# Who asks for the output stores of the lower tiles: GpSimd in place of SyncE

## The chip, the cores and the metric

The kernel runs on one core of a Trainium2 chip. The time of a run is the time on the device, in microseconds. It was run three times before the change: the median is 1073.89 us, the lowest 1072.86 and the highest 1074.72. One execution was also recorded by the hardware profiler; that one took 1074.23 us, and the profile that is read below is of that execution.

The core has engines that run their own instruction streams in order and wait for each other on semaphores: PE (TensorE, matrix products), DVE (VectorE), ACT (ScalarE), POOL (GpSimd) and SP (SyncE). In this kernel SP computes nothing, it only asks for transfers (DMAs). ACT and POOL can ask for them too. The transfers themselves run on the core's 16 DMA engines.

## The reference

Eight sequences (B) of 576 tokens (S), eight heads (H) of 64 (D), all in float32. Attention is confined to chunks of 64 tokens. Its output is mixed by the real part of a two-dimensional Fourier transform, added to itself, normalised, and sent through an MLP of 512 to 2048 to 512 without biases:

```python
scores = scale * np.matmul(q_c, k_c.transpose(0, 1, 2, 4, 3))      # per chunk of 64 tokens
attn = np.exp(scores - max); attn = attn / (sum(attn) + 1e-09)
x = (attn @ v_c)            # regrouped to (8, 576, 512)
u = x + np.real(fft(fft(x, axis=1), axis=2))
un = (u - mean(u)) / np.sqrt(var(u) + 1e-06)
out = u + np.maximum(un @ w_ch1, 0.0) @ w_ch2
```

## The kernel before, in words

**Tiles.** The 576 tokens of a sequence are nine chunks of 64. A tile holds 128 tokens. For the Fourier transform over the tokens, chunks are paired from both ends: a LO tile (lower) holds two chunks of the first half of a sequence, a HI tile holds the mirrored chunks of the second half, and a RE tile holds the middle chunks of two sequences. So there are 16 LO tiles, 16 HI tiles and 4 RE tiles. Rows within a tile are ordered by odd and even tokens, for the LO tiles from the end of a chunk to its start.

**Groups.** The MLP goes over nine groups (`g` from 0 to 8). Groups 0 to 7 hold the four tiles of one sequence, in the order LO, HI, LO, HI (`groups[g]`). The last group holds the four RE tiles. While PE works on the MLP of a group, the attention and the Fourier mix of the next sequence (`attention(b)`, `fourier(b)`) are woven in between as side work, step by step at due times, in the loop at the end of the kernel.

**The order.** Every instruction stands in the order in which the program text issues it (`tc.manual_schedule`); nothing is moved by a planner. Each engine takes its own instructions in that order.

**The MLP.** Group 0 uses the weights as they are (`up_first`, `down_plain`). Later groups multiply in halves of 256 with seven products in place of eight (`up_halves`, L1265, whose matmuls are line 1289, and `down_halves`, L1319, whose matmuls are line 1341). The combinations of weights that this needs are made once, kept in DRAM (`s1`, `s2`, `s3`), and fetched slab by slab (`fetch`, L1151: L1155 for the first product's weights, L1160 for the second's, 1 MB each). For group 1 they are made in place by POOL: `keep1`, line 1069, four operations for each of four pairs of weight blocks, in the steps that begin at the end of group 0. The last group has its own products (`down_few`), and POOL makes their weights in `make_rest` (line 1133).

**The ends of a group.** In group 0 all four tiles are finished in the last step of `down_plain`: DVE adds the residual (L1249) and `store` (L1030) is called. In groups 1 to 7, `down_halves` finishes the tiles in four steps: the first LO tile and then the first HI tile after the sixth product (`o == 5`, DVE at L1358), the second LO tile and then the second HI tile after the seventh (DVE at L1361). The outputs lie in `os_`, a part of the weight buffer `wb` that is shared with `xs`, an operand of the next group (written by DVE at L1167).

**The store.** For each of a tile's two chunks `store` asks for the DMAs that bring its rows back into the order of tokens:

- a LO tile: one DMA for each chunk, 64 rows of 2 KB, 128 KB, at line 1037. Since rows are kept in the order odd and even, from the end, the DRAM side is written as two interleaved sequences of 32 rows: its sizes are 2 x 32 x 512.
- a HI tile: two DMAs for each chunk, 32 rows each, 64 KB, line 1046, one by SP and one by ACT.
- a RE tile: lines 1040 to 1042.

**What shares SP with it.** SP also loads q and k (`load`, L250, four DMAs for a tile) and v (`load_v`, L273), fetches the slabs, and keeps `s1` (`keep1_store`, L1074). The loaded q and k are transposed by DVE (L416, into `qT` and `kT`) before PE makes the scores (L448); for a LO tile POOL then copies a column of `qT` (L418). The attention's output is divided by its sum by DVE (L511 to L515), and a few of its rows are moved by POOL (`shift`, L555; L526).

**Completion semaphores.** The DMAs that SP and ACT ask for share eight completion semaphores, taken in turn in the program's order. So one such DMA can be issued only after the eighth one before it has landed. The DMAs that POOL asks for have eight of their own. The groups before the last put twelve stores into the rotation of SP and ACT: four of LO tiles (SP), four of HI tiles by SP and four by ACT.

Of the kernel before, what the change touches and what calls it, by code (L numbers as in the profile page):

```python
# [16 lines left out]
def kernel(  # L17
# [32 lines left out]
    nc = tc.nc  # L50
# [3 lines left out]
    CH = 64  # L54
# [140 lines left out]
    def kind(n):  # L195
        return tiles[n][0]
# [4 lines left out]
    def chunks(n):  # L201

        what, b, i = tiles[n]
        if what == RE:
            return [(b, NC // 2), (b + 1, NC // 2)]
        if what == LO:
            return [(b, 2 * i), (b, 2 * i + 1)]
        return [(b, NC - 1 - 2 * i), (b, NC - 2 - 2 * i)]
# [821 lines left out]
    def store(n, o):  # L1030

        last = n in groups[-1][1::2]
        for h, (b, c) in enumerate(chunks(n)):
            r0, t0 = h * CH, c * CH
            if kind(n) == LO:
                to = out[b, t0 + 1:t0 + CH + 1, :][::-1].rearrange("(i r) d -> r i d", r=2)[::-1]
                nc.sync.dma_start(out=to, in_=o[r0:r0 + CH])
            elif kind(n) == RE:
                eng = nc.scalar if last and h else nc.sync
                eng.dma_start(out=out[b, t0 + 1:t0 + CH:2, :], in_=o[r0:r0 + ODD])  # L1040
                eng.dma_start(out=out[b, t0 + 4:t0 + CH:2, :], in_=o[r0 + ODD + 2:r0 + CH])
                eng.dma_start(out=out[b, 0:t0 + 3:t0 + 2, :], in_=o[r0 + ODD:r0 + ODD + 2])
            else:
                for r in range(2):
                    eng = nc.scalar if r else nc.sync
                    eng.dma_start(out=out[b, t0 + 1 - r:t0 + CH:2, :], in_=o[r0 + ODD * r:r0 + ODD * r + ODD])
# [182 lines left out]
    def down_plain(g, h1):  # L1229
# [4 lines left out]
        for m in range(KF):  # L1234
            for s, dn in enumerate(dns):
                nc.tensor.matmul(  # L1236
                    out=dn,
                    lhsT=h1[:, m, s * 128:(s + 1) * 128],
                    rhs=w2[:, m, :],
                    start=(m == 0),  # L1240
                    stop=(m == KF - 1),
                )
                if m == KF - 1:
                    n = groups[g][s]
                    if s < G - 1:
                        o = three_p.tile([128, DM], FP32, tag="o", name="o")
                    else:
                        o = one_p.tile([128, 2 * (HM + 1)], FP32, tag="two", name="o")[:, 0:DM]
                    nc.vector.tensor_tensor(out=o, in0=dn, in1=natural(n), op=ALU.add)  # L1249
                    store(n, o)  # L1250
            for j in range(G):
                due = KF - (G - j + 1)
                if m == due - 2:
                    normed(g + 1, j)
                if m == due:
                    turned(g + 1, j)
                    if j >= 2 and g + 1 >= first_of[1]:
                        combined(g + 1, j - 2)
            yield
# [59 lines left out]
    def down_halves(g, h1):  # L1319
        pas, pbs = {}, {}  # L1320
        for o in range(NO):
            w = slab2[((g - first_of[2]) * NO + o) % NS2]
            for r in range(2):
# [21 lines left out]
                if o == 0:  # L1345
                    nc.scalar.copy(a, dst)
                elif o == 1:
                    nc.vector.tensor_tensor(out=b, in0=dst, in1=a, op=ALU.add)
                elif o == 2:
                    nc.vector.tensor_tensor(out=a, in0=dst, in1=b, op=ALU.add)  # L1350
                elif o == 3:
                    nc.vector.tensor_tensor(out=ohigh[:, HM:DM], in0=dst, in1=ohigh[:, HM:DM], op=ALU.add)
                    nc.gpsimd.tensor_tensor(out=olow[:, HM:DM], in0=b, in1=natural(low)[:, HM:DM], op=ALU.add)
                    nc.gpsimd.tensor_tensor(out=ohigh[:, 0:HM], in0=b, in1=natural(high)[:, 0:HM], op=ALU.add)
                elif o == 4:
                    nc.vector.tensor_tensor(out=olow[:, 0:HM], in0=dst, in1=natural(low)[:, 0:HM], op=ALU.add)
                elif o == 5:
                    nc.vector.tensor_tensor(out=olow[:, HM:DM], in0=dst, in1=olow[:, HM:DM], op=ALU.add)  # L1358
                    store(low, olow)
                else:  # L1360
                    nc.vector.tensor_tensor(out=ohigh[:, 0:HM], in0=dst, in1=ohigh[:, 0:HM], op=ALU.add)  # L1361
                    store(high, ohigh)
# [254 lines left out]
```

## Time and profile before

| what | value |
|---|---|
| median of three runs | 1073.89 us |
| the profiled execution | 1074.23 us |
| its span (first to last instruction) | 1072.2 us |
| PE busy | 1046.3 us, 98% |
| DVE busy | 610.8 us, 57% |
| POOL busy | 406.6 us, 38% |
| ACT busy | 315.3 us, 29% |
| HBM traffic | 177.31 MB read, 34.08 MB written, 197 GB/s over the span |
| SP's and ACT's DMAs | 208.04 MB and 2.76 MB |
| POOL's DMAs | 0.66 MB |

The profile is of one execution. Busy time leaves out the instructions that only issue DMAs, which is why SP has no row. The span is 2.0 us shorter than the profiled execution's time; that part lies before the first and after the last instruction. Line numbers (L1037) are those of the kernel. In the list of waits a line says which engine and operation waited, for whom, and then the microseconds in total, how often, and the longest. In a timeline the first number is the start in microseconds from the start of the span, the second the length, and the end of the line, in brackets, is how long the engine was idle before and what ended it. In the chain of waits, each piece is followed back from the last instruction to what released it.

### The profile page before, as it was taken

To read this page: it belongs to the slowest core of one execution; us is meant where nothing else is said; L and a number is where in the kernel's file an instruction comes from. 1 tells how busy PE (TensorE), PEld (TensorE's weight loads), DVE (VectorE), ACT (ScalarE), POOL (GpSimd) and SP (SyncE) were. 2 spreads that over 40 slices of the span, in tenths; PEclk is the share of its full clock that TensorE was granted. 3 is DMA by queue.
4 is the path that set the end of the run, shared out by engine and by line. 5 is a ranking of instruction groups with operands and counts; after the bars stand their busy time and mean duration, and the time that the engine had idled before them with its cause. 6 is when DMAs were issued, how large, how long until landed. Compare 5 with 4: busy or idle time off the path is not lost.

```text
span 1072.2 us, 20212 instructions
## 1 busy us (share of the span) xinstructions
PE 1046.3 (98%) x7498; PEld 854.6 (80%) x7498; DVE 610.8 (57%) x1319; ACT 315.3 (29%) x746; POOL 406.6 (38%) x531
## 2 busy tenths in 40 slices
PE   8999989899999999999999999999999999999997
PEld 6645444688888888888888888788888888888886
DVE  4798986684567465664565554745664535433331
ACT  4688563233113411322032312331133103101200
POOL 4310018672415140344134321614161726780281
PEclk9999999999999999999999999999999999999999
DMA  8767565489668546883667266954654559776763
GB/s 176 232 186 218 123 196 189 139 249 312 233 199 232 149 140 198 239 232 119 191 209 231 99 182 195 231 165 163 202 177 116 208 191 350 229 231 199 272 228 106
DMA packets 157759, 212.74 MB, mean 198 GB/s; under 512 B 69308, under 2 KB 103100, under 8 KB 151390
## 3 DMA queue, kind: packets, MB, share of 16 engines
q1 hardware_dynamic: 154012, 208.04, 63.4%
q10 hardware_dynamic: 3330, 2.76, 1.1%
q8 instruction: 60, 0.98, 0.4%
q0 software_dynamic: 320, 0.66, 0.3%
q14 instruction: 37, 0.30, 0.1%
HBM read 177.31 MB, written 34.08 MB: 197 GB/s over the span
## 4 chain that ended last, share of the span: by engine, by line
PE 77%; DVE 8%; DMA 5%; ACT 4%; SPq 3%; issue 2%; POOL 1%; DVEq 0%; ACTq 0%; POOLq 0%
PE pa L1289 19%; PE pb L1341 18%; PE pb L1289 14%; PE pa L1341 13%; PE dn L1405 4%; PE pt L397 2%; PE mix L838 2%; DMA xall<-in_moe_w_ch_dram 1%; SPq L263 1%; PE xp L498 1%; PE z L719 1%; DVE power L378 1%; DMA out_dram<-o 1%; PE sc L448 1%; DMA v<-in_v_dram 1%
## 5 line engine op out<-in xcount | busy, mean ns | idle before, releaser
L1289 PE MATMUL pa<-unT,wa 128*128 128x256 f32 x736 | 175.0, 381 | 2.5 <-DVE wa L1297 2.5
L1289 PEld LDWEIGHTS pa<-unT,wa 128*128 128x128 f32 x736 | 138.3, 190 | 21.8 <-DVE wa L1297 2.7
L1289 PE MATMUL pb<-wa 128*128 128x256 f32 x448 | 106.9, 381 | 0.1
L1341 PE MATMUL pa<-wb,h 128*128 128x256 f32 x448 | 101.5, 380 | 0.0
L1341 PE MATMUL pb<-wb,h 128*128 128x256 f32 x448 | 100.7, 379 | 0.0
L1289 PEld LDWEIGHTS pb<-wa 128*128 128x128 f32 x448 | 84.1, 190 | 12.3 <-DVE h L1299 0.5
L1341 PEld LDWEIGHTS pa<-wb,h 128*128 128x128 f32 x448 | 83.9, 190 | 11.3
L1341 PEld LDWEIGHTS pb<-wb,h 128*128 128x128 f32 x448 | 84.1, 190 | 11.0
L1169 POOL TENSOR_TENSOR h<-h 128x256 f32<-128x256 f32 x56 | 47.7, 860 | 102.3 <-DVE wb L1167 98.2
L555 POOL COPY xall<-xall 1x512 f32<-1x512 f32 x28 | 17.8, 636 | 154.3 <-DVE xall L515 126.9
L1295 DVE TENSOR_TENSOR wa<-pb,wa 128x256 f32<-128x256 f32 x56 | 23.8, 425 | 69.7 <-ACT wa L1294 69.7
L1289 PE MATMUL pb<-unT,wa 128*128 128x256 f32 x256 | 60.5, 379 | 0.0
L1303 ACT ACTIVATE h<-pa 128x256 f32<-128x256 f32 x64 | 24.6, 384 | 114.1 <-PE pa L1289 113.6
L1236 PE MATMUL dn<-wb,h 128*128 128x512 f32 x128 | 57.5, 597 | 0.0
L1294 ACT COPY wa<-pa 128x256 f32<-128x256 f32 x56 | 20.9, 372 | 123.5 <-PE pa L1289 80.6
L1289 PEld LDWEIGHTS pb<-unT,wa 128*128 128x128 f32 x256 | 48.6, 190 | 6.6
L1289 PE MATMUL pa<-wa 128*128 128x256 f32 x224 | 53.9, 383 | 0.0
L1309 ACT ACTIVATE h<-h 128x512 f32<-128x512 f32 x64 | 39.6, 629 | 45.0 <-DVE h L1308 44.8
L1341 PE MATMUL pb<-wb,yall 128*128 128x256 f32 x224 | 51.2, 381 | 0.0
L1341 PE MATMUL pa<-wb,yall 128*128 128x256 f32 x224 | 50.6, 379 | 0.3 <-DMA wb<-s 0.3
L1341 PE MATMUL pb<-wb 128*128 128x256 f32 x224 | 50.7, 379 | 0.0
L1195 PE MATMUL up<-unT,wa 128*128 128x512 f32 x108 | 49.4, 598 | 0.0
(299 smaller groups left out, 1976.1 us busy)
## 6 DMA issues: line engine op xcount, KB each, us to landing
wb<-s SPq DMA_DIRECT2D x49, 1024.0 KB
wa<-s SPq DMA_DIRECT2D x196, 256.0 KB
xall<-in_moe_w_ch_dram SPq DMA_DIRECT2D x22, 512.0 KB
q<-in_q_dram SPq DMA_DIRECT2D x96, 112.0 KB
k<-in_k_dram SPq DMA_DIRECT2D x96, 112.0 KB
wb<-s SPq DMA_DIRECT2D x16, 512.0 KB
v<-in_v_dram SPq DMA_DIRECT2D x124, 64.0 KB
s<-part SPq DMA_DIRECT2D x30, 256.0 KB
```

Of the source, the lines that this page charges most:

```text
L397: nc.tensor.transpose(pt[:, j, :], src(j), ident)
L838: nc.tensor.matmul(out=mix[:, cols], lhsT=zt[:, T], rhs=tab, start=(T == 0), stop=(T == 3), skip_group_check=True,)
L1169: nc.gpsimd.tensor_tensor(out=h1[:, m, hi], in0=h1[:, m, lo], in1=h1[:, m, hi], op=ALU.subtract)
L1195: nc.tensor.matmul(out=up, lhsT=w1[:, kk, m * 128:(m + 1) * 128], rhs=unT[:, kk], start=(kk == 0), stop=(kk == KD - 1), skip_group_check=True,
L1236: nc.tensor.matmul(out=dn, lhsT=h1[:, m, s * 128:(s + 1) * 128], rhs=w2[:, m, :], start=(m == 0), stop=(m == KF - 1),)
L1289: nc.tensor.matmul(out=dst, lhsT=w[:, kk, r], rhs=rhs[o][:, kk], start=(o in (0, 1) and kk == 0), stop=(kk == 1), skip_group_check=True,)
L1294: nc.scalar.copy(a, dst)
L1295: nc.vector.tensor_tensor(out=b, in0=pbs[r][:, 0], in1=a, op=ALU.add)
L1303: nc.scalar.activation(out=h1[:, m, lo], in_=dst, func=ACTF.Relu)
L1309: nc.scalar.activation(out=h1[:, HF + m], in_=h1[:, HF + m], func=ACTF.Relu)
L1341: nc.tensor.matmul(out=dst, lhsT=lhs[:, m], rhs=w[:, m], start=(o in (0, 2) and m == 0), stop=(m == HF - 1), skip_group_check=True,)
L1405: nc.tensor.matmul(out=dst, lhsT=lhs[:, m], rhs=w[:, m], start=(fresh and not half and m == 0), stop=(m == 3), skip_group_check=True,)
```

## The change

The DMA that stores a chunk of a LO tile is issued by GpSimd (POOL) in place of SyncE. What it transfers, from where and to where, is the same. The stores of HI and RE tiles stay as they are.

```diff
@@ -1034,7 +1034,7 @@
             r0, t0 = h * CH, c * CH
             if kind(n) == LO:
                 to = out[b, t0 + 1:t0 + CH + 1, :][::-1].rearrange("(i r) d -> r i d", r=2)[::-1]
-                nc.sync.dma_start(out=to, in_=o[r0:r0 + CH])
+                nc.gpsimd.dma_start(out=to, in_=o[r0:r0 + CH])
             elif kind(n) == RE:
                 eng = nc.scalar if last and h else nc.sync
                 eng.dma_start(out=out[b, t0 + 1:t0 + CH:2, :], in_=o[r0:r0 + ODD])
```

There are 16 LO tiles of two chunks, so 32 DMAs change their engine, four in each of the groups 0 to 7. They leave SP's instruction stream and the rotation of eight completion semaphores that SP and ACT share, and stand in POOL's stream at the place where `store` is called; they use POOL's own completion semaphores. The order of the instructions on PE, DVE and ACT is the same as before.

## The prediction

> **What bounds the kernel now.** I read the page first. TensorE (PE) is busy for 98% of the span at full clock, so a change that only moves who issues a DMA can win no more than the time in which PE stands still and the store is the reason. The page also shows that POOL, the engine that receives the work, has room.
>
> ```profile
> span 1072.2 us, 20212 instructions
> PE 1046.3 (98%) x7498; PEld 854.6 (80%) x7498; DVE 610.8 (57%) x1319; ACT 315.3 (29%) x746; POOL 406.6 (38%) x531
> ```
>
> Second, the waits from the first changed store (about 189 us) to the end. Only these three of PE are long:
>
> ```profile
> PE pa L1289 <- DVE wa L1297: 2.5, 1, 2.5
> PE pb L1289 <- POOL wb L1069: 2.4, 1, 2.4
> PE sc L448 <- DVE kT L416: 0.7, 1, 0.7
> ```
>
> I also took PE's starts in order and counted what each gap has over the usual spacing. The same places cost 2.66 us (at 670.4 us), 2.78 (189.8) and 0.88 (211.4), and then 0.42 (218.8), 0.74 (222.5) and 0.41 (260.7) follow; nothing else after 189 us is over 0.3. The 2.78 ends in front of the first changed store and stays. So at most 0.88 + 0.42 + 0.74 + 0.41 + 2.66 = 5.1 us can be won.
>
> Third, what stands behind those gaps. The chain of waits around 200 us, and around 660 us, in order of time (start, length, what):
>
> ```profile
> 195.48 7.65 DMA out_dram<-o
> 203.15 0.34 SPq L250
> ...
> 204.01 7.00 DMA k<-in_k_dram
> ...
> 211.13 0.06 DVE kT L416
> ```
>
> ```profile
> 657.88 8.90 DMA v<-in_v_dram
> 666.78 0.02 issue
> 666.80 4.80 DMA q<-in_q_dram
> ...
> 671.80 0.06 DVE qT L416
> ```
>
> A store (`out_dram<-o`, L1037) takes 7.65 us to land, a load of k waits for it and itself takes 7.00, and DVE's transpose waits for the load. The timeline of SP around 655 us shows how the second chain starts:
>
> ```profile
> 649.78 5.84 SPq L1037 DMA_DIRECT2D out_dram<-wb  x2
> 655.72 0.83 SPq L1046 DMA_DIRECT2D out_dram<-wb  x2
> 656.65 0.38 SPq L1160 DMA_DIRECT2D wb<-s  x1
> 657.13 3.59 SPq L273 DMA_DIRECT2D v<-in_v_dram  x4
> 662.40 4.77 SPq L250 DMA_DIRECT2D q<-in_q_dram  x4
> ```
>
> Two stores take 5.84 us of SP because the second waits for a landing, and everything behind it on SP is late by that. DVE's timeline gives the end of both chains, with its idle time in brackets:
>
> ```profile
> 211.13 1.09 DVE L416 STREAM_TRANSPOSE kT<-k 128x512 f32<-128x512 f32 x1 [3.74 <-DMA k<-in_k_dram]
> 671.80 1.09 DVE L416 STREAM_TRANSPOSE qT<-q 128x512 f32<-128x512 f32 x1 [4.12 <-DMA q<-in_q_dram]
> ```
>
> **What the Trainium skill says.** All of this is on its page "DMA: Bandwidth & Descriptors". (1) "Why a DMA increments its semaphore by 16 and not by 1": a DMA uses k engines, the largest k up to 16 that divides the outermost sizes of both sides, and on SP's path always the lowest-numbered k. The lower store's DRAM side is 2x32x512, so k = 2. The trace agrees: each L1037 moves its semaphore in 3 steps, all other DMAs of SP in 16, and while only L1037 is in flight the 16 engines are about 0.1 busy at 12 to 18 GB/s. It lands in 6.90 us in the median (5.29 to 10.43), the upper stores of 64 KB each (L1046) in 5.65. Loads of k issued behind lower stores took 7.0 to 7.9 us, others with none ahead (217.74 to 219.37) 2.6 to 2.9. From POOL, the section says, either such DMAs go to all 16 engines or to k engines that rotate; no trace here shows which. (2) "Queues, rings and completion order": each queue has its own ring on each engine, and an engine alternates between rings. So a store in POOL's ring no longer stands ahead of SP's loads in one line, though it still shares the engine. (3) "Issuing engines are not separate DMA queues": the bytes run on the same 16 engines, so nothing is won in bandwidth. (4) "Specifications": the first byte comes after about 1 us from POOL against 0.6 from SP. That is less than the landing spread here, and nobody waits for these stores but their buffers (below).
>
> **The change part by part.**
>
> *Removed.* 32 DMAs leave SP, 4 in each of the 8 full groups: about 0.52 us each (28 with median 0.520, four with 0.582), together 17 us of SP's issue time, plus 28 us of waiting in front of them (the largest entries are 19.9 for DVE L1358 and 11.2 for landings). SP isn't the bound on average, so this counts only where SP's next load is late.
>
> *Moved past.* SP's and ACT's DMAs share eight completion semaphores in rotation, so each waits until the eighth before it has landed. A group's stores put 12 DMAs into that rotation before, 8 after. Each wait now falls on another DMA. I worked out the pairs from the program's order.
>
> At 195 to 211 us (end of group 0): before, k waits for the store issued at 195.48 (landed 203.14), is issued at 203.15 to 204.01, and lands at 210.05 to 211.01. After, its slots belong to q loads landed by 196.6, so DVE's release of the old k at about 198.4 decides: issued 198.4 to 200, and at 3 to 5 us landed about 203. DVE was free for it at 207.4, so its 3.74 us of idle time goes. The next work on DVE, L511, needs attention's output from PE (210.9 to 211.5), so DVE doesn't gain 3.7 us but the transpose's 1.09, run earlier. PE's 0.88 goes with it; of the 0.42 and 0.74, which come from DVE's backlog, a part. Bounds 0.9 and 2.0; I take 1.2.
>
> At 649 to 671 us (end of group 4): after, the upper stores stand where the lower ones stood, at 649.8. The second waits for a slab fetch issued at 647.14 (fetches land in 4.64 to 9.21, median 5.24; so about 652.5). Then fetch at 653, v at 653.5 to 656, q at 657.5 to 659.5, landed about 664. DVE could take it at 671.80 - 4.12 = 667.7, so 3.7 us of margin, and the stall of 2.66 goes whole. If that fetch takes 9.2 us, q comes 4 us later and about 0.3 of the stall is left.
>
> At 260.7 us a slab is late by 0.41 because SP issues without a pause from 244 to 257. With four DMAs less in that group SP runs ahead; I take 0.3 (0 to 0.41).
>
> *Added.* 32 DMA issues on POOL. Its only direct row is
>
> ```profile
> L273 POOL DMA_DIRECT2D v<-in_v_dram x10 | 6.3, 633 | 0.6 <-DMA v<-in_v_dram 0.4 <-issue 0.2
> ```
>
> so 0.63 us each, 32 x 0.63 = 20 us, on an engine 38% busy. That row is of another shape, so I bound one issue by 0.5 (SP's) and 1.5 us. Behind them in POOL's order:
> - Group 0: four DMAs stand between two sets of L1069. What PE needs of the set behind them was ready at 198.13, is ready 4 x 0.63 = 2.5 us later, at 200.6, and is used by PE at 207.33. Cover 207.33 - 198.13 = 9.2 us, gone above 9.2/4 = 2.3 us for each DMA.
> - Groups 1, 3, 5: four DMAs before row copies (L555). The last wait (DVE L1361) ends at 306.5, so POOL is free at 307.8, three copies of 0.64 end at 309.7, and the fourth waits for DVE until 312.07 anyway. Cover 2.3 us, then 15 us of idle time (L526, to 329.08).
> - Groups 2, 4: two DMAs ahead of a small copy for qT (638.7), which PE uses at 648.7; two ahead of copies that wait for 650.34 (POOL is through with the DMAs at 646.5, with the first two copies at 648). Cover 10 and 2 us.
> - Groups 6, 7: between additions (L1133) for the last group; POOL's next work that PE needs is at 997. Cover over 10 us.
>
> So this adds 0 to PE within my bounds.
>
> *Waits added.* POOL now waits for DVE's L1358 and L1361, in the groups above, and what is queued behind is what I listed. The lower rows' buffer is rewritten by DVE (L1167) at 331.5, 444.9, 892.6 and so on; a store issued by 307.8 with even 10.4 us to land is through by 318.2. Cover 13 us. The end of the kernel has no such store.
>
> *Sum.* 1.2 + 2.66 + 0.3 = 4.2 us. The profiled execution took 1074.23 (span 1072.2 plus 2.0 around it), so 1070.0. The median is 1073.89, 0.34 lower, so **1069.7 us**.
>
> **The rivals.**
>
> *The gain is taken back by the rotation (no change).* With SP running earlier, another DMA takes the place of the store in a wait: the slab fetch of 647.14, or upper stores of 9 to 10 us. Then only group 0's 1.2 us are won, or a new gap of 1 to 2 us eats the rest: 1074.23 - 1.2 = 1073.0 in the profile, 1072.7 as median. For it: eight semaphores still serve q, k, v, slabs and upper stores, and fetches have a long tail. Against it: 3.7 us of margin.
>
> *POOL's issue is dear (slower).* POOL could need several microseconds for a DMA while DVE is busy beside it. For it: two additions of one size, L1169 and L1353 (128x256), take 860 and 725 ns, so POOL's pace isn't constant. At 4 us each, four cost 16 us, which is 16 - 9.2 = 6.8 us of PE at group 0; groups 1, 3 and 5 lose nothing more (what their copies lack is followed by 15 idle us). Against the 4.2 won that is +2.6, so 1073.89 + 2.6 = 1076.5. It decides from (9.2 + 4.2)/4 = 3.4 us a DMA up. Against: the row with 0.63, which is five times less.
>
> *The transfers matter, not the issue.* If two engines are clogged as before, whoever asks, loads behind stay at 7 us. Then at group 0 k still starts 4 us earlier and lands 207; at group 4 q lands at about 667.5: nearly the same gain, 3.7 us, 1070.2. It lies in the forecast's range.
>
> **How the numbers follow.** Forecast with the third rival: 0.66, range 1068.3 to 1071.3 (bounds 0.9 + 2.4 + 0 = 3.3 and 2.0 + 2.66 + 0.41 = 5.1 us, plus 0.7 for other small gaps and the runs' spread). Taken back: 0.18, 1071.7 to 1075. Dear issue, or one new stall of that size: 0.16, 1076 to 1080. The kernel's measurement tells 0.2%, or 2.15 us, from no change: faster means below 1071.7, slower above 1076.0. For 8 in 10 the range takes the first and the second case: 1068.0 to 1075.5.
>
> **What would show it.** Right: at 200 to 211 us k is issued before 201 and DVE's idle time before kT is gone; at 670 us PE's wait for L1297 is gone; the POOL DMAs of L1037 are at 0.5 to 1 us; L1069 moves by 2.5 us without a wait of PE. Wrong: a PE wait for POOL's L1069 near 207, a wait on the slab fetch at 650, or a new late slab in the groups' first halves, where SP's earlier loads meet slab fetches.

## The result, and the profile after

The changed kernel took 1071.53 us in the median of ten runs (1068.75 to 1073.07), beside 1073.99 us for the kernel before in ten runs (1071.62 to 1076.28). The ratio is 0.997, with a 95% interval of 0.996 to 0.998: 2.5 us faster. Forecast were 1069.7 us, 4.2 us faster. The time lies in the stated range and on the stated side, but the gain is six tenths of what was forecast. Repeated later in 14 runs, the changed kernel took 1070.69 us beside 1073.70, ratio 0.9974 (0.9964 to 0.9984).

The profiled execution of the changed kernel took 1068.75 us, with a span of 1067.0. That is 5.5 us under the profiled execution of before, more than twice the difference of the medians. Why the two profiles differ by more than the kernels do is a main finding below.

The page of the kernel after, first lines:

```profile
span 1067.0 us, 20226 instructions
PE 1044.8 (98%) x7498; PEld 854.8 (80%) x7498; DVE 610.8 (57%) x1319; ACT 315.4 (30%) x746; POOL 429.6 (40%) x563
```

POOL has 32 instructions more (531 to 563) and 23.0 us more busy time (406.6 to 429.6). PE, DVE and ACT have as many instructions as before. Of PE's three long waits after 189 us, one is left in the list of waits:

```profile
PE pb L1289 <- POOL wb L1069: 2.4, 1, 2.4
```

It is the one in front of the first changed store, 2.78 us over the usual spacing as before. The timeline of SP around the end of group 4 (start, length, what) shows how the chain that began with two stores of 5.84 us has gone:

```profile
647.31 2.25 SPq L1046 DMA_DIRECT2D out_dram<-wb  x2
652.63 0.34 SPq L1160 DMA_DIRECT2D wb<-s  x1
653.08 2.64 SPq L273 DMA_DIRECT2D v<-in_v_dram  x4
655.81 1.03 SPq L1155 DMA_DIRECT2D wa<-s  x2
656.93 2.35 SPq L250 DMA_DIRECT2D q<-in_q_dram  x4
```

q is asked for from 656.93, not from 662.40, and landed at 662.9, not at 671.6. DVE's timeline at the two places, with no idle time before qT and 0.35 us before kT:

```profile
207.37 1.12 DVE L416 STREAM_TRANSPOSE kT<-k 128x512 f32<-128x512 f32 x1 [0.35 <-DMA k<-in_k_dram]
...
665.94 1.10 DVE L416 STREAM_TRANSPOSE qT<-q 128x512 f32<-128x512 f32 x1
```

The stores themselves, in the view of line 1037 (durations in ns, lowest, median and highest; first and last start in us):

```profile
L1037 POOL DMA_DIRECT2D out_dram<-wb x28: 662/662/708, 297.7 to 966.1; - x28
L1037 POOL DMA_DIRECT2D out_dram<-o x4: 662/672/724, 195.1 to 197.2; - x4
  DVE wb L1358: 81.8, 7
  DVE wb L1361: 35.6, 7
DMA to landing us min/median/max: 5.9/7.7/9.2
```

One issue on POOL is 0.66 to 0.67 us, and POOL waits for DVE before them; no wait of PE follows from that in this trace. The store takes 7.7 us to land, longer than from SP (6.90 in the median). So the stores did not become faster. SP's upper stores did, from 5.65 to 4.78 us in the median. Loads of q and k did not on the whole: their median after 189 us is 3.87 us here and 4.22 in a second trace of this kernel, and 4.24, 3.95 and 4.08 in three traces of the kernel before. At the end of group 4 what SP asks for behind its stores did land sooner: the slab fetch after 5.33 us and v after 4.3 to 5.3, where they took 9.21 and 7.1 to 9.2.

### The profile page after: what moved, and what is told of

The parts are those of the page before. It is cut to its first block, busy times and chain, and to the rows that moved or that the text cites. A ratio compares the mean times of both kernels' runs of the same rounds, so it can differ in the third digit from the quotient of the medians.

```text
span 1067.0 us, 20226 instructions
## 1 busy us (share of the span) xinstructions
PE 1044.8 (98%) x7498; PEld 854.8 (80%) x7498; DVE 610.8 (57%) x1319; ACT 315.4 (30%) x746; POOL 429.6 (40%) x563
## 4 chain that ended last, share of the span: by engine, by line
PE 84%; DVE 5%; ACT 4%; DMA 2%; SPq 2%; POOL 1%; issue 1%; ACTq 0%; DVEq 0%; POOLq 0%
PE pa L1289 21%; PE pb L1341 18%; PE pb L1289 16%; PE pa L1341 14%; PE dn L1405 4%; PE pt L397 3%; PE mix L838 2%; PE xp L498 2%; PE z L719 1%; PE sc L448 1%; SPq L263 1%; PE up L1195 1%; DVE power L378 1%; PE dn L1236 1%; DMA yall<-in_moe_w_ch_dram 1%
## 5 line engine op out<-in xcount | busy, mean ns | idle before, releaser
L1037 POOL DMA_DIRECT2D out_dram<-wb x28 | 18.8, 674 | 118.0 <-DVE wb L1358 81.8
L1294 ACT COPY wa<-pa 128x256 f32<-128x256 f32 x56 | 20.8, 372 | 124.3 <-DMA out_dram<-wb 68.0
```

## The experiments

My theory was that the gain consists of two chains of waits, one at the end of group 0 and one at the end of group 4, both starting with a lower store. Rivals were that the gain is spread over all groups, that the rotation of eight semaphores carries it and not the slow landing, and that POOL's side sets a bound. The kernel before took 1073.62 us in 35 runs beside the first four of these kernels, 1073.59 in nine beside the next, and 1073.70 in 19 beside the last.

**One chain at a time.** Only group 0 on POOL:

```diff
-                nc.sync.dma_start(out=to, in_=o[r0:r0 + CH])
+                eng = nc.gpsimd if b == 0 else nc.sync
+                eng.dma_start(out=to, in_=o[r0:r0 + CH])
```

> Only the four lower stores of group 0 go to POOL; the other 28 stay on SP. My theory (two chains of waits, one at the end of group 0 and one at the end of group 4): the gap of 0.88 us before the scores at 211 us is gone and part of the two that follow it, so 1.0 to 1.3 us faster than before, about 1072.8; PE's wait of 2.5 us for L1297 at 670 us is still there. Rival (the gain is spread over all groups, because SP is relieved everywhere): an eighth of the 2.5 us between the medians, 0.3 us.

Measured: 1073.02 us, ratio 0.9993 (0.9984 to 1.0003). It isn't told from no change. 1.0 to 1.3 us were expected; 0.6 is the difference of the medians. PE's gap before the scores at 211 us isn't in its trace. That alone says little: PE's clock was low there (0.66 of full speed from 195 to 200 us), and with a low clock the kernel before doesn't have that gap either, as is shown below. The two gaps that follow it are there (0.37 and 0.73 us), so they don't hang on a wait of PE for k. PE's wait for L1297 is there, though shorter than in the first trace.

Only group 4 on POOL (`b == 4` in place of `b == 0`):

> Only the four lower stores of group 4 go to POOL. My theory: PE's wait of 2.5 us for L1297 at 670 us is gone and nothing else changes, so 2.7 us faster in the profile, about 1071.3; the 0.88 us at 211 stays. If the wait at 670 is not in most runs of the kernel before, but only in some, the medians differ by less than the profiles do. Rival (spread over all groups): 0.3 us.

Measured: 1071.99 us, ratio 0.9982 (0.9974 to 0.9991), so 1.6 us between the medians, with no wait of PE for L1297 in its trace. The chain of group 4 is most of the gain, and 1.6 is less than the 2.66 us that one trace showed. The expectation's own clause (the wait differs from run to run) fits; two more traces of the kernel before, below, bear it out. That the gain is spread evenly (0.3 us) is excluded by this interval.

**What makes the chains: a store on few DMA engines.** The stores stay on SP, as many as before and in the same places of the rotation; only the form of the DRAM side changes. The kernel leaves out that rows are brought back into the order of tokens:

```diff
-                to = out[b, t0 + 1:t0 + CH + 1, :][::-1].rearrange("(i r) d -> r i d", r=2)[::-1]
+                to = out[b, t0 + 1:t0 + CH + 1, :]
                 nc.sync.dma_start(out=to, in_=o[r0:r0 + CH])
```

> All lower stores stay on SP, as one DMA each of the same 128 KB, in the same place of the rotation of eight semaphores; only the form of the DRAM side is changed to 64 consecutive rows, so that its outermost size is 64 and not 2. The rows of these tiles are thus stored in the wrong order (same bytes, same buffers). If the cause of both chains is that a store of two engines lands late (5.3 to 10.4 us): landing in the trace takes 2 to 5 us, with 16 semaphore steps; k at the end of group 0 is issued before 201, both gaps of PE are gone, and the time is that of the changed kernel, 1069 to 1071.5. If the cause is the issue by SP and the twelve stores in the rotation, whatever the landing: both gaps stay and the time is 1074.

Measured: 1070.86 us, ratio 0.9969 (0.9959 to 0.9979): the whole gain of the change, without moving a store. In its trace L1037 lands in 2.44 us in the median (2.24 to 5.02) and not in 6.90; its semaphore moves in 16 steps, not in 3. SP's upper stores next to it land in 1.79 us in place of 5.65, though nothing in them was changed. PE has no wait for L1297 in this trace, and k at the end of group 0 has landed by 203.9. So the Trainium skill's rule on the number of engines ("DMA: Bandwidth & Descriptors", "Why a DMA increments its semaphore by 16 and not by 1") fits the case: by it the 128 KB go through two engines with an outermost size of 2, and through 16 with 64. Behind the store on two engines, what SP asked for next landed late too. The form also changes the order of the addresses, from every second row to consecutive rows. That this alone makes the difference is unlikely: the upper stores take every second row as well, and they land in 1.79 us here. SP's timeline of this kernel at the end of group 4:

```profile
646.64 6.40 SPq L1037 DMA_DIRECT2D out_dram<-wb  x2
653.14 1.00 SPq L1046 DMA_DIRECT2D out_dram<-wb  x2
654.23 0.38 SPq L1160 DMA_DIRECT2D wb<-s  x1
654.71 2.77 SPq L273 DMA_DIRECT2D v<-in_v_dram  x4
...
658.69 2.65 SPq L250 DMA_DIRECT2D q<-in_q_dram  x4
```

The two stores still hold SP for 6.40 us, because the second waits for the landing of an upper store of ACT (652.55). So the time for which the two stores hold SP, which the prediction put first, isn't what made q late. SP is through with them at 653.0, 2.6 us earlier than before, but q lands 6.7 us earlier. Most of that lies in the landings behind the stores: the slab fetch that follows lands after 5.79 us and v after 4.4 to 5.6, where they took 9.21 and 7.1 to 9.2 before, and q, which must wait for those landings, is issued and landed in time (664.95).

The same on POOL:

```diff
-                to = out[b, t0 + 1:t0 + CH + 1, :][::-1].rearrange("(i r) d -> r i d", r=2)[::-1]
-                nc.sync.dma_start(out=to, in_=o[r0:r0 + CH])
+                to = out[b, t0 + 1:t0 + CH + 1, :]
+                nc.gpsimd.dma_start(out=to, in_=o[r0:r0 + CH])
```

> The changed kernel, with the DRAM side of the lower stores as 64 consecutive rows (rows stored in the wrong order, same bytes), so that its outermost size is 64 and not 2. If the slow landing of a store from POOL is that of few DMA engines: landing falls from 7.7 us to 3 or less, the loads of k behind it at the end of group 0 land in 3 us and not in 5 to 8, and DVE's idle time of 0.35 us before kT is gone; but PE gains at most 0.3 us, since it doesn't wait there any more: 1071.0 to 1071.6. If POOL spreads both forms in the same way: landing stays at 7 to 8 us.

Measured: 1069.96 us, ratio 0.9964 (0.9952 to 0.9977). That is below the 1071.0 to 1071.6 that were expected, but it overlaps with the changed kernel's 0.997 (0.996 to 0.998), so no further gain is shown. The view of line 1037 in this kernel ends with the landing:

```profile
DMA to landing us min/median/max: 2.2/3.2/6.2
```

3.2 us against 7.7 with the other form. From POOL too the form decides, although here the semaphore takes 16 steps in both forms, so its steps don't tell on how many engines such a store runs. And one issue takes 0.54 us in place of 0.66. The four loads of k at the end of group 0 land after 2.3 to 2.4 us, where they took 5.0 to 8.3 in the changed kernel, and DVE no longer waits for k. So the slow stores delay SP's loads from POOL's queue too.

**Another engine that shares the rotation.** ACT in place of POOL:

```diff
-                nc.sync.dma_start(out=to, in_=o[r0:r0 + CH])
+                nc.scalar.dma_start(out=to, in_=o[r0:r0 + CH])
```

> All lower stores are asked for by ACT in place of SP: they leave SP's stream and SP's rings, but stay in the rotation of eight semaphores and on two engines. If the rotation carries the delay (a load waits for a store's landing): k at the end of group 0 is still issued after 202 and the 0.88 us at 211 stay; at 670 at least 1 us of the 2.66 stays, so 1072.5 to 1074. If SP's stream and rings alone carry it: both gaps are gone, 1069 to 1071.5. ACT is held by the stores' own waits, up to 8 us at group ends as its upper stores show, so a new wait of PE for ACT would make it 1075 to 1080.

Measured: 1082.68 us, ratio 1.0082 (1.0069 to 1.0096): 9 us slower, beyond the worst that I gave. ACT's timeline in this kernel, around the end of group 4:

```profile
652.53 1.08 ACTq L1037 DMA_DIRECT2D out_dram<-wb  x2
656.05 5.20 ACTq L1046 DMA_DIRECT2D out_dram<-wb  x2
661.35 0.65 ACT L1294 COPY wa<-pa 128x256 f32<-128x256 f32 x2 [9.23 <-DMA q<-in_q_dram]
```

ACT stands in its stores until 661.25, and then makes the copies L1294 that PE waits for; the list of PE's waits has them at several group ends:

```profile
PE pa L1289 <- ACT wa L1294: 4.8, 3, 2.0
...
PE pa L1289 <- ACT xall L1294: 1.7, 1, 1.7
PE pt L397 <- ACT ex L474: 1.5, 3, 0.5
```

The store lands in 8.18 us here. At the end of group 0 SP's upper stores wait in the rotation from 201.20 to 206.68, and k goes out from 206.78 on, 4 us later than in the first trace of before. But it lands after 2.3 us, by 210.5, earlier than the 211.0 of that trace, since no lower store is in flight any more. So what I expected of the rotation (k late, PE's gap kept) was wrong: k issued late behind no store was there before k issued early behind stores. What the run shows besides: ACT has work on PE's path, it waited for landings, and PE waited for it.

**How much cover POOL has.** The changed kernel with more work on POOL behind the four DMAs of group 0:

```diff
-            nc.gpsimd.tensor_tensor(out=out_, in0=in0, in1=in1, op=op)
+            for _ in range(11 if pair == 1 and out_ is o1 else 1):
+                nc.gpsimd.tensor_tensor(out=out_, in0=in0, in1=in1, op=op)
```

> The changed kernel, with the first operation of the second set of L1069 (o1 = a21 + a22, at the end of group 0, right behind the four DMAs on POOL) done eleven times in place of once; the repeats write the same values. Ten repeats of 1.27 us are 12.7 us more of POOL ahead of what PE needs. In the changed kernel that is ready at 200.5 and used by PE at 207.0, so 6.5 us of cover are left by my theory: PE waits 12.7 - 6.5 = 6.2 us at 207 us, and the time is 6 us over the changed kernel's, 1077 to 1078. Rival (the four DMAs already use up the cover, or POOL's work here is waited for by somebody else first): 9 us or more over it. Rival (it is hidden wholly): the same time as the changed kernel.

Measured: 1077.71 us (1077.56 to 1078.23), ratio to the kernel before 1.0036 (1.0023 to 1.0050), 6.2 us over the changed kernel's first median. PE's timeline in this kernel:

```profile
214.19 3.78 PE L1290 MATMUL pb<-xall,wb 128*128 128x256 f32 x8 [5.36 <-POOL wb L1070]
```

(its lines are one further down). The eleven operations took 14.80 us on POOL where one takes 1.29, so 13.5 us were added, and 5.53 us of them came out as a gap (over the usual spacing). Of the other 8.0 us, 1.7 were hidden because PE itself came later, at 208.66 and not at 206.96: its clock was at half for 3.41 us from 192.3 on. That leaves 6.3 us of cover after the DMAs, where 6.5 was worked out. The step that put POOL's issue at nothing holds, and so does its limit.

**All stores on POOL.** LO and HI tiles, beside the change:

```diff
-                    eng = nc.scalar if r else nc.sync
+                    eng = nc.gpsimd
```

> All stores of LO and HI tiles on POOL, 12 DMAs in a group and none of them in the rotation of SP and ACT. If every store that leaves the rotation helps: faster than the changed kernel by up to 1 us (1070.5). By my theory nothing more is to be won, since after the change no wait of PE stands behind a store; at the end of group 0 the twelve DMAs of 0.67 us are 8.0 us, which puts POOL's second set at 206, an inch before PE's 207: 1071.5, or up to 2 us more if POOL's waits for DVE come in between; and the loads of k and q behind the HI stores land no earlier.

Measured: 1070.06 us, ratio 0.9964 (0.9951 to 0.9978), under the 1071.5 of my theory. A second time, beside the changed kernel:

> The changed kernel once more, on one chip beside the next one. 1071.0 to 1071.8, 2.2 to 3 us under the kernel before; in its trace no wait of PE at 670 us and none for kT.

> All stores of LO and HI tiles on POOL, a second time, beside the changed kernel. Its first trace had no gap of PE over 0.3 us after 190 us, where the changed kernel has 0.36 and 0.73 at 217 and 221 us: if these 1.1 us are its gain it is 0.5 to 1.5 us under the changed kernel here. If the difference of the first time was between sessions only: within 0.4 us of it.

Measured: 1070.69 us for the changed kernel, ratio 0.9974 (0.9964 to 0.9984), and 1069.87 us with all stores on POOL, ratio 0.9960 (0.9947 to 0.9974). Both times the second is lower, by 0.8 us here, but the intervals overlap, so that it is better than the change isn't shown. Its traces show two effects that offset each other. In the second one PE waits 1.96 us at 206.8 for POOL's L1069, which stands behind twelve DMAs; POOL itself waits 2.63 us for a landing between them. In the first one PE doesn't wait: its clock was at half for 3.41 us from 193.3 on, and it came later. And in both, the gaps at 217 and 221 us, which the changed kernel kept (0.36 and 0.73), are gone. Their cause can be read from DVE's timeline there. The changed kernel:

```profile
214.84 1.47 DVE L1167 TENSOR_TENSOR wb<-h 128x256 f32<-128x256 f32 x1
216.35 1.37 DVE L1168 TENSOR_TENSOR yall<-wb,h 128x256 f32<-128x256 f32 x1
```

With all stores on POOL:

```profile
216.22 0.41 DVE L1167 TENSOR_TENSOR wb<-h 128x256 f32<-128x256 f32 x1
216.67 0.71 DVE L1168 TENSOR_TENSOR yall<-wb,h 128x256 f32<-128x256 f32 x1
```

The same operation of DVE takes 1.47 us beside POOL's L1069 (POOL has it from 214.77 to 220.26 in the changed kernel), and 0.41 us beside POOL's row copies L555 (216.31 to 219.36 in the other). The kernel with the repeated L1069 differs from the changed kernel in POOL's work alone, and shows both cases in one trace, POOL first and then DVE (lines one further down):

```profile
222.33 2.63 POOL L555 COPY xall<-xall 1x512 f32<-1x512 f32 x4
225.02 0.71 POOL L555 COPY xall<-first 1x512 f32<-1x512 f32 x1
225.81 1.32 POOL L1070 TENSOR_TENSOR wb<-wa 128x512 f32<-128x512 f32 x1
```

```profile
224.84 0.42 DVE L1168 TENSOR_TENSOR wb<-h 128x256 f32<-128x256 f32 x1
226.26 1.15 DVE L1168 TENSOR_TENSOR wb<-h 128x256 f32<-128x256 f32 x1
```

0.42 us beside the row copies, 1.15 beside the additions, and no gap of PE at this place. The Trainium skill names such a contention ("GPSIMD Engine Reference", "1. Specifications": POOL shares its access to SBUF with VectorE, and instructions of DVE with two inputs in SBUF contend); L1167 has two such inputs. The trace agrees for POOL's additions; beside the row copies, which are POOL's work too, it shows no slowing. So, as far as these traces show, the two gaps come from what POOL does then, not from the load of k.

**How constant the gaps of before are.** The kernel before, unchanged, two more times with a trace:

> The kernel before once more, for a second trace of it. If the wait of PE for L1297 at 670 us is fixed by the order of the program, it is again 2.5 us (the other trace with that code in group 4, that of group 0 alone on POOL, has 1.2). If it hangs on how long a few transfers take, it is anything from 0 to 4 us, and the 0.88 us at 211 is there in any case, give or take 0.5.

> The kernel before, a third trace. The wait of PE for L1297 near 670 us is there, 1 to 3 us. The 0.88 us before the scores at 211 us are there only if the granted clock is full from 190 to 200 us; if it is lower there, as in the second trace, PE comes to the scores 1 to 2 us later and k is there in time.

Measured: 1073.87 and 1075.27 us. The wait of PE for L1297 near 670 us in the lists of waits of these two traces:

```profile
PE pa L1289 <- DVE wa L1297: 1.7, 1, 1.7
```

```profile
PE pa L1289 <- DVE wa L1297: 0.7, 1, 0.7
```

So it is there each time, but 2.5, 1.7 and 0.7 us long. The gap of 0.88 before the scores at 211 us is in neither trace. The windows of the first trace and of the second show why (the window and its length, then PE's, PEld's, DVE's, ACT's and POOL's busy us and instructions, then the granted clock, the DMA share and GB/s). The kernel before, first trace:

```profile
195.00:200.00 5.00, 5.00 (x26) 4.40 (x26) 2.98 (x6) 1.33 (x3) 4.92 (x5) 1.00 0.38 84
```

Second trace:

```profile
195.00:200.00 5.00, 5.00 (x21) 4.15 (x21) 1.21 (x4) 1.29 (x3) 4.92 (x4) 0.77 0.35 86
```

In the second trace the clock is 0.77 here (0.66 in the third). It was at half for one stretch of 3.41 us, from 193.8 on (195.5 in the third), which costs PE 1.7 us. PE then comes to the scores at 213.82 and not at 212.28, and k's transpose, done at 213.08, is in time (in the third trace it is done at 215.43, and PE comes at 215.59). So in these traces the 0.88 us are a cost only where the clock stays full at 195 us, as it did in the one that was profiled first. The clock tells besides why the third trace has the smallest gaps and the longest time: there it was at half for 6.83 us from 11.2 on as well.

The mean granted clock is known for 24 runs of the changed kernel and 63 of the kernel before, and in the mean it is 0.997 for both, so a luckier clock isn't the gain. Sorted by it, the medians are 1069.5 us (8 runs) and 1072.9 (16 runs) at 0.999 or more, 3.4 us apart, and 1071.7 (15) and 1073.9 (27) at 0.996 or less, 2.2 us apart. The sorting was done afterwards and nothing set the clock, but it fits: where the clock stays full, the kernel before has more to lose.

## Why the prediction was right and wrong, point by point

**The end of group 4 (2.66 us, whole).** The place and the cure were right: no trace of a kernel with group 4 on POOL has that wait. What it is worth was mis-sized. Its gap of PE over the usual spacing is 2.66, 1.91 and 0.90 us in three traces of the kernel before, and 1.34 in the kernel with only group 0 moved: 1.7 in the mean, and 1.6 us is what the change of group 4 alone measured. The forecast took one execution for all.

**The end of group 0 (1.2 us).** This step failed. The 0.88 us are in one of three traces of before. And "of the 0.42 and 0.74, which come from DVE's backlog, a part" was wrong: DVE is slow there because POOL's L1069 runs beside it, and not because k is late. They stay at 0.36 to 0.38 and 0.73 to 0.74 in both traces of the changed kernel. By its time, group 0 alone is told neither from nothing nor from 1.2 us (0.6 us, interval from 1.7 faster to 0.3 slower); it is the traces that show which parts weren't there.

**260.7 us (0.3 us).** The gap of 0.41 is gone in the trace after, but the two other traces of before don't have it either, so it was worth less.

**The sum.** All gaps of PE of over 0.15 us after 202 us add up to 7.8, 5.4 and 4.8 us in the three traces of the kernel before (mean 6.0), and to 3.5 and 3.7 us in the two of the changed kernel (mean 3.6). The means differ by 2.4 us, and the medians of the first comparison by 2.5. The first trace alone gives 7.8 - 3.5 = 4.3, which is the forecast's 4.2. So the working fits the execution that it was made from, and that execution had larger gaps than the others and a full clock at 195 us. With three and two traces, both of the changed kernel with a full clock, the agreement of the means is a rough one. And the stated range held because it was 3 us wide: the terms together were 1.7 us too large.

**The reason inside the chains.** The prediction named both the slow landing on two engines and the waits in the rotation. The store in another form, which keeps the rotation, has the whole gain, so the slow landing is where the chain begins. But the change itself doesn't cure it (7.7 us from POOL). There SP's loads are issued earlier, since no lower store stands ahead of them on SP or in the rotation; which of these two counts for more was not separated. At group 0 the prediction had k landed at 203; it landed at 207.25, as its third rival said (207): issued up to 4 us earlier, k still took 5.0 to 8.3 us beside POOL's slow stores. The 4 us cost nearly nothing because DVE was busy until 207.0. At group 4 SP's order came out as forecast, and q landed at 662.9 (forecast 664).

**POOL's cost (0).** Right. One issue is 0.67 us where 0.63 was taken. What PE needs of L1069's second set was ready at 200.5 (forecast 200.6), and the extra work showed 6.3 us left. The rival of a dear issue is refuted.

**The other rivals.** A new wait that takes the gain back (no change) wasn't seen: no gap over 0.3 us is in the traces after that is not in those before.

**Slips in the working.** SP's waiting in front of the lower stores is not 28 us: the list of waits has 39.5 (19.9, 11.2, 7.5 and 0.9). By its own terms the range begins at 1068.1 us, not at 1068.3. And L1037 is not alone in moving its semaphore in few steps: ten other DMAs of SP (L299, L306, L1042) have two to five. None of this changes the forecast of 1069.7 us.

## What to carry to other kernels

Look at the outermost size of a transfer's access pattern before looking at who asks for it: a store on two DMA engines delayed what stood behind it, and a form with 64 rows outside gave the same gain as the move to another queue. That form is no replacement here, since it leaves the rows in the wrong order; two DMAs of 32 rows for each chunk, as the HI tiles have, would keep the order, and no run tried them. When a gain is read from gaps of a microsecond, take several traces: a gap that depends on landing times and on the granted clock may be three times as long in one execution as in the next. A queue whose engine has idle time and separate completion semaphores (here POOL) was a good place for a slow store, and an engine that works on the path (here ACT) a bad one.

## What had not been expected

- In nine of the thirteen traces the granted clock falls to half for 3.41 us, beginning between 191.8 and 195.5 us, and in four it stays full there. A slower PE hides a late load.
- A lower store lands no faster from POOL (7.7 us in the median) than from SP (6.9), but SP's upper stores do (4.78 in place of 5.65), and so does what SP asks for behind them at the end of group 4.
- DVE's addition of 128x256 takes 0.41 us in one kernel and 1.15 to 1.48 us in another, depending on which work of POOL runs beside it.
- With the stores on ACT the kernel is 9 us slower: ACT waits for landings, and PE for ACT.
